# Two layer joints laid out anew: which tiles of the attention layer lie under which tiles of the recurrent layer, and in which order SyncE issues the last weight loads and the last stores

## The chip, the cores and the metric

The kernel runs on one core of a Trainium2 chip. The metric is the time of one execution on the device in microseconds (us); the median of several executions is compared.

## The reference

The program is a stack of four layers on 2048 tokens of width 640, each added to its input: A, B, A, B. Both A layers use the same weights, and so do both B layers.

```python
x = x + A(layernorm(x)); x = x + B(layernorm(x))
x = x + A(layernorm(x)); x = x + B(layernorm(x))
# A: 4 segments of 512 tokens, 32 heads of 20: causal softmax attention in the segment,
#    mixed by a gate with a linear-attention memory M, z carried over the segments; then o @ wo
# B: 64 segments of 32 tokens, 32 heads of 128
for s in range(64):
    h = concat([mem, x[32*s:32*s+32]])           # 8 memory tokens and 32 tokens
    q, k, v = h @ Wq, h @ Wk, h @ Wv
    o = softmax(mask(q @ k.T * scale)) @ v
    o = o @ Wo
    mem, out[s] = o[:8], o[8:]
```

## The kernel before, in words

**Layer A** (`layer_A`) works through 32 groups (4 segments of 8 groups of 4 heads). At its end the last segment's 512 tokens are finished as four row blocks of 128 tokens, numbered 0 to 3: `out_stage_b` multiplies each by the output weights `a_wo` (tile `a_YP`), adds the residual `a_xr` on VectorE into a 32-bit row block, stores that to the DRAM tile `xres` (line 408), makes a 16-bit copy in a slice of the tile `a_Onat` on ScalarE (line 414), and stores that to `xres_bf` (line 417). The text calls the eight stores x0, b0, x1, b1, x2, b2, x3, b3, in this order. In the first A layer the 32-bit blocks stand in `a_xnew` (block 0), `a_late` (1 and 2) and `a_xnew3` (3, in pool `a_am`); in the second in the two buffers of `a_xr` (0 and 1) and in `a_late` (2 and 3). `C.rows` holds the last eight stores.

**Layer B** (`layer_B`) is a chain of 64 steps. In a step TensorE projects K and Q (`b_Ka`, `b_Qa`, `b_Kb`, `b_Qb`, `b_Qc`), computes scores (`b_SP`) and V (`b_Va`, `b_Vb`); VectorE and ScalarE make the softmax, in which ScalarE writes `b_E` (`soft_exp`), VectorE sums it, GpSimd scales it into `b_Pn`, VectorE transposes that to `b_PTa`, `b_PTb`; TensorE then forms `b_OTP`, which goes through `b_OTsb` into 64 matmuls with the output weights (`b_OPS`). The result's first rows are the memory of the next step, so no step starts its projections before the one ahead has its `b_OPS`. In B all engines but SyncE keep the order in which the program is written (`_OrdNC`).

**Output weights of B** are eight tiles `b_wo0` to `b_wo7` of 640 KB. `WO_FIRST` = 0, 4, 1, 5, 3 is loaded first, `WO_LAST` = 7, 2, 6 last (line 889), which is the order in which `b_OPS` reads them. All loads and stores around the joints are issued by SyncE, one after the other; an issue that has to wait holds up all behind it. At a joint, order-only dependencies put the five loads of `WO_FIRST` ahead of all eight stores.

**SBUF.** Each layer opens its pools in a fixed order, and they lie one behind the other. A layer's pools begin where the pools of the layer ahead began, so each tile lies on tiles of that layer, and its first write waits until their last reader is done; the last reader can be a DMA that stores them.

Of the kernel before, what the change touches and what calls it, by code (L numbers as in the profile page):

```python
# [19 lines left out]
BF16 = mybir.dt.bfloat16  # L20
# [62 lines left out]
def layernorm_begin(nc, pool, C, xt, name):  # L83
    stats = pool.tile([128, 2, nc.vector.BN_STATS_DIM], F32, name=f"{name}_st", tag="ln_st")
    first = nc.vector.bn_stats(out=stats[:, 0, :], in_=xt[:, 0:320])
    nc.vector.bn_stats(out=stats[:, 1, :], in_=xt[:, 320:640])
    mv = pool.tile([128, nc.vector.BN_AGGR_DIM], F32, name=f"{name}_mv", tag="ln_mv")
    nc.vector.bn_aggr(out=mv[:], in_=stats[:])
    rstd = pool.tile([128, 1], F32, name=f"{name}_rstd", tag="ln_rstd")
    nc.vector.tensor_scalar(out=rstd[:], in0=mv[:, 1:2], scalar1=LN_EPS, scalar2=None, op0=ALU.add)  # L90
    nc.gpsimd.tensor_tensor(out=rstd[:], in0=rstd[:], in1=C.mhalf[:, 0:1], op=ALU.pow)
    return first, mv, rstd
# [175 lines left out]
def layer_A(nc, tc, C, W, x_src, x_dst, src_is_bf16, nseg=4, out_bf16=False, xb_dst=None, load_w=None, side_loads=None):  # L268
# [7 lines left out]
    with ExitStack() as ctx:  # L276
        def pool(name, bufs):
            return ctx.enter_context(tc.tile_pool(name=name, bufs=bufs, reuse_waits="tile"))
# [13 lines left out]
        wk = pool("a_wk", 2)  # L292
        w1 = pool("a_wk1", 1)
        stm = pool("a_stm", 1)
        pam = pool("a_am", 3)
        pon = pool("a_on", 2)
        wkl = pool("a_wkl", 2)
        w1l = pool("a_wk1l", 1)
        st = pool("a_state", 1)
        sm = pool("a_sm", 4)  # L300
        W.wo = st.tile([128, NCH, D], BF16, name="a_wo")

        def psum(name, bufs):
# [11 lines left out]
        vaug = [stm.tile([128, 4, 4, 32], BF16, name=f"a_vaug{i}") for i in range(4)]  # L315
        Kn = [stm.tile([128, 4, 4, 32], BF16, name=f"a_Kn{i}") for i in range(2)]
        phik = [ste.tile([128, 4, 4, 32], BF16, name=f"a_phik{i}") for i in range(2)]
        NM = [stm.tile([128, 4, 4, 32], BF16, name=f"a_NM{i}") for i in range(2)]

        def pads(i, eng):  # L320
            for on, dst, k in ((i < 2, Kn, 0), (True, vaug, 1)):
# [264 lines left out]
        def negmax_rows(g):  # L586
            nm, N_ = GS[g]["nm"], NM[g % 2]
            K("NM1").gpsimd.tensor_copy(N_[:, :, :, 20], nm[:])
            K("NM2").gpsimd.tensor_tensor(out=N_[:, :, :, 21], in0=nm[:], in1=N_[:, :, :, 20], op=ALU.subtract)

        def q_with_max(g):
            s_ = GS[g]
            N_ = NM[g % 2]
            Q2 = pg.tile([128, 512], F32, name="a_Q2", tag="pg")
# [111 lines left out]
        for i in range(2):  # L706
            P.memset(NM[i][:], 0.0)
            if i == 0:
# [99 lines left out]
        for g in range(NGR + 2):  # L808
            n, G = divmod(g, 8)
            for half in range(2):  # L810
                p, tp = 2 * g + half, 2 * g + half - 3
                for ph in range(2):
                    K.base = 4 * g + 2 * half + ph
                    todo = []
                    for what in VISITS[ph]:
                        kind, r = what[0], int(what[1])
# [10 lines left out]
                    for step in range(2):  # L827
                        for kind, p_, r, X, o0 in todo:
                            if step == 0 and g >= NGR and (kind, p_) != ("T", 2 * NGR - 3):
                                tail_unit(*next(PARTS))  # L830
                            f = (s_mm, s_max)[step] if kind == "S" else (t_round, t_exp)[step]
# [27 lines left out]
WO_FIRST, WO_LAST = (0, 4, 1, 5, 3), (7, 2, 6)  # L859
# [28 lines left out]
def load_B_wo(nc, W, B_Wo, k):  # L888
    return nc.sync.dma_start(W.wo[k][:], B_Wo[4 * k:4 * k + 4].rearrange("h e d -> e h d"))
# [8 lines left out]
def layer_B(nc, tc, C, W, x_src, xb_src, x_dst, mem0, B_Wv, B_Wo, nsteps=64, out_bf16=False, tag=""):  # L898
# [6 lines left out]
    with ExitStack() as ctx:  # L905
        def pool(name, bufs):
            return ctx.enter_context(tc.tile_pool(name=name, bufs=bufs, reuse_waits="tile"))
# [14 lines left out]
        for nm, ks in (("b_wo", WO_FIRST[0:3]), ("b_xo", ()), ("b_wom", WO_FIRST[3:]), ("b_wol", WO_LAST)):  # L922
# [4 lines left out]
            for k in ks:  # L927
                W.wo[k] = p_.tile([128, 4, D], BF16, name=f"b_wo{k}")
        wkl = pool("b_wkl", 1)
        wk = pool("b_wk", 1)  # L930
        sm = pool("b_sm", 2)

# [6 lines left out]
        def ps_tile(shape, dtype, name):  # L939
            return pp.tile(shape, dtype, name=name, tag="ps")  # L940
# [45 lines left out]
        def ln_begin(key, after=None):  # L986
            xt = ln_xt[key]
            f, mv, rstd = layernorm_begin(nc, sml, C, xt[:], "b_ln")
            if after is not None:
                info = mybir.DependencyInfo(mybir.DependencyClass.NoSync, mybir.DependencyReason.SCHED_ONLY)  # L990
                tc.add_manual_dep(f.ins, after.ins.name, info, reason="order")
            ln_open.append((key, xt, mv, rstd))

        def ln_end():
            if ln_open:
                key, xt, mv, rstd = ln_open.pop()
                if key[0] == "X":
                    ln_xt[key] = bx.tile([128, D], BF16, name="b_xn", tag="xt")
                layernorm_end(nc, xt[:], mv, rstd, ln_xt[key][:])
                ln_ready.append(key)  # L1000
# [16 lines left out]
        def cols_of(u):  # L1017
            return HX[u // 4][:, :, u % 4, :]
# [91 lines left out]
        for k in WO_FIRST + WO_LAST:  # L1110
            f = load_B_wo(nc, W, B_Wo, k)
            if k == WO_FIRST[-1]:
                for r in C.rows:
                    tc.add_manual_dep(r.ins, f.ins.name, mybir.DependencyInfo(mybir.DependencyClass.NoSync, mybir.DependencyReason.SCHED_ONLY), reason="order")
        ln_begin(("H", 0), C.after)
        ln_end()
        nc.vector.memset(Pn[:], 0.0)
# [74 lines left out]
        for s in range(nsteps):  # L1192
# [38 lines left out]
            negmax = sm.tile([128, 2, 5], F32, name="b_negmax", tag="negmax")  # L1231
            ssum = sm.tile([128, 2, 5], F32, name="b_ssum", tag="ssum")
            rs = sm.tile([128, 2, 5], F32, name="b_rs", tag="rs")
            E_ = wk.tile([128, 2, 5, 40], BF16, name="b_E", tag="E0")

            def soft_max(b, SP):
                nc.vector.tensor_reduce(out=negmax[:, b, :], in_=SP[:], axis=AX.X, op=ALU.max, negate=True)
# [4 lines left out]
            def soft_exp(b, SP):  # L1242
                nc.scalar.activation(out=E_[:, b], in_=SP[:], func=ACT.Exp)

            def soft_sum(b):
                nc.vector.tensor_reduce(out=ssum[:, b, :], in_=E_[:, b], axis=AX.X, op=ALU.add)

# [3 lines left out]
            def soft_p(eng, b):  # L1251
                eng.tensor_tensor(out=Pn[:, b, :, 0:40], in0=E_[:, b], in1=rs[:, b, :].unsqueeze(2).to_broadcast([128, 5, 40]), op=ALU.mult)

# [16 lines left out]
            def vtail_some(n_):  # L1270
                nonlocal vps, vc
                if work and vc < NCH:
                    vps = vtail_unit(work[0], work[1], vc, min(NCH, vc + n_), vps)
                    vc = min(NCH, vc + n_)
# [85 lines left out]
            order = [(0, 0), (0, 1), (1, 0), (1, 1), (3, 0), (3, 1), (2, 0), (2, 1)]  # L1360
# [8 lines left out]
            vtail_some(1)  # L1369
            if not last:  # L1370
                dst = cols_of(s + 1)
                msb = wk.tile([128, 320], BF16, name="b_msb", tag="msb")
                parts = ((0, 1), (1, 3), (3, NCH))
                for ca, cb in parts:
                    nc.scalar.copy(msb[:, 64 * ca:64 * cb], ops[:, 64 * ca:64 * cb])
                for pi, (ca, cb) in enumerate(parts):
                    mt = ps_tile([128, cb - ca, 8], F32, f"b_MT{pi}")
                    for c in range(ca, cb):
                        for q in range(4):
                            o = 64 * c + 32 * (q % 2)  # L1380
                            nc.tensor.matmul(mt[32 * q:32 * q + 32, c - ca, :], lhsT=msb[:, o:o + 32], rhs=selm[:, q // 2, :],
                                             start=True, stop=True, tile_position=(0, 32 * q), skip_group_check=True)
                    nc.vector.tensor_copy(dst[:, ca:cb, 24:32], mt[:])
                    vtail_some((1, 1, NCH)[pi])
# [24 lines left out]
def full_kernel(tc, A_x, A_wq, A_wk, A_wv, A_wo, A_beta, B_x, B_mem0, B_Wq, B_Wk, B_Wv, B_Wo, B_seg_len, out, layers="ABAB"):  # L1409
    nc = tc.nc  # L1410
    with ExitStack() as ctx:
        C, WA = alloc_consts(tc, ctx)
        xin = A_x.rearrange("b s d -> (b s) d")
        xout = out.rearrange("b s d -> (b s) d")
        mem0 = B_mem0.rearrange("b t d -> (b t) d")
        X = tc.dram_tile([S_TOK, D], F32, name="xres")
        Xb = tc.dram_tile([S_TOK, D], BF16, name="xres_bf")
        WB = C.WB = alloc_B_resident(tc, ctx)
        padded = {}
        stage = {nm: t_[:, k, 0:NCH * D].rearrange("p (c n) -> p c n", c=NCH)  # L1420
                 for nm, t_, k in (("wq", WB.wq, NCH - 1), ("wk", WB.wk, NCH - 1), ("wv", WB.wq, NCH - 2))}
        build_consts(nc, tc, C)
        nl = len(layers)
        assert layers[0] == "A" and layers[-1] == "B"
        for li, L in enumerate(layers):
            lastl = (li == nl - 1)
            if L == "A":
                first = li == 0

                def side(slot, after):  # L1430
                    if slot % 3 == 1 and slot // 3 < 8 * NCH:
                        load_B_resident(nc, WB, B_Wq, B_Wk, slot // 3, after)
                    if slot == 24:
                        keep_padded(nc, tc, WA, padded)

                layer_A(nc, tc, C, WA, xin if first else X, X, first, xb_dst=Xb,
                        load_w=lambda: load_A_weights(nc, tc, C, WA, A_wq, A_wk, A_wv, A_wo, padded, stage),
                        side_loads=(side, A_beta) if first else None)
            else:
                layer_B(nc, tc, C, WB, X, Xb, xout if lastl else X, mem0, B_Wv, B_Wo, out_bf16=lastl, tag=str(li))  # L1440
# [58 lines left out]
```

## Time and profile before

| | us |
|---|---|
| median of 3 runs (lowest, highest) | 2403.32 (2401.88, 2407.49) |
| profiled execution: device time | 2403.94 |
| profiled execution: span of the instructions | 2401.9 |
| first joint, A to B | about 330 to 365 in the span |
| second joint, A to B | about 1527 to 1558 in the span |

Times in the profile are microseconds from the start of the span. A row of the timeline reads: start, length, engine, line, operation, output<-inputs, shapes, count, and in brackets the idle time of the engine before it and what ended it. "SPq" rows are issues of DMAs by SyncE; their length is the time of issuing, not of the transfer. Line 114 is a helper through which most instructions are recorded, so tiles' names tell more than lines.

### The profile page before, as it was taken

What the parts mean: (1) busy time and instruction counts of PE and PEld (TensorE: products, weight loads), DVE (VectorE), ACT (ScalarE), POOL (GpSimd) and SP (SyncE); (2) the same over time, 40 slices, a digit from 0 to 9 for tenths busy, and PEclk for the clock granted to TensorE, in tenths of its full rate; (3) what the DMA queues carried; (4) which work ended last, traced back from release to release, by engine and by line L of the source; (5) the groups of instructions that cost most, each with busy time, mean ns of one, the idle gap of its engine ahead of it and who ended that gap; (6) DMA issues with size and microseconds to landing.
All of it is one profiled execution on the core that took longest, in us unless ns stands there. A gap on an engine that the chain in (4) does not pass through costs nothing.

```text
span 2401.9 us, 139146 instructions
## 1 busy us (share of the span) xinstructions
PE 2274.9 (95%) x62200; PEld 1491.3 (62%) x62264; DVE 1882.6 (78%) x4701; ACT 1414.2 (59%) x3194; POOL 749.2 (31%) x1590
## 2 busy tenths in 40 slices
PE   8999989999999999999989999899999999999998
PEld 5566655666666666666656665566666666666665
DVE  9999876777777777777789998777777777777776
ACT  6999964445444445444479999644544444444443
POOL 6677741111111111111146776311111111111111
PEclk9999999999999999999999999999999999999999
DMA  5122271111111111111130211711111111111110
GB/s 169 50 86 67 72 255 25 29 33 29 32 29 30 31 31 32 29 29 29 45 113 19 68 51 34 270 25 26 28 29 26 28 27 27 27 29 28 27 23 21
DMA packets 173186, 123.37 MB, mean 51 GB/s; under 512 B 106652, under 2 KB 157740, under 8 KB 171052
## 3 DMA queue, kind: packets, MB, share of 16 engines
q1 hardware_dynamic: 172162, 114.44, 16.6%
q8 instruction: 486, 7.96, 1.4%
q14 instruction: 112, 0.92, 0.1%
q10 hardware_dynamic: 426, 0.05, 0.0%
HBM read 79.60 MB, written 34.80 MB: 48 GB/s over the span
## 4 chain that ended last, share of the span: by engine, by line
PE 70%; DVE 14%; ACT 9%; DMA 3%; issue 3%; POOL 1%; SPq 0%; ACTq 0%; POOLq 0%; DVEq 0%
PE b_OPS L114 11%; PE b_Ka L114 6%; PE b_Qa L114 6%; PE b_Kb L114 6%; DVE a_nm L143 5%; PE b_tail L114 5%; PE b_Vb L114 5%; PE b_Va L114 5%; ACT a_PT L143 4%; PE b_vtail L114 3%; PE b_OPSd L114 3%; PE b_SP L114 3%; PE a_S L114 3%; PE b_OTP L114 2%; PE b_Qb L114 2%
## 5 line engine op out<-in xcount | busy, mean ns | idle before, releaser
L114 POOL TENSOR_TENSOR b_Pn<-b_E,b_rs 128x200 bf16<-128x200 bf16 x256 | 133.5, 522 | 1084.7 <-DVE b_rs L114 1067.0
L143 DVE TENSOR_REDUCE a_nm<-a_S 128x2 f32<-128x512 f32 (+3 forms) x512 | 395.0, 815 | 44.4 <-PE a_S L114 29.3
L143 ACT ACTIVATE a_PT<-a_T 128x1024 bf16<-128x1024 f32 (+1 forms) x384 | 345.7, 905 | 23.4 <-PE a_T L114 16.5
L114 PEld LDWEIGHTS <-b_HX 128*32 128x32 bf16 x9200 | 239.1, 96 | 140.0 <-DVE b_HX L114 3.0
L114 PEld LDWEIGHTS <-b_R 128*32 128x32 bf16 x8960 | 231.9, 96 | 138.9 <-DVE b_R L114 3.1
L114 PE MATMUL b_OPS<-b_wo,b_OTsb 128*32 128x320 bf16 x8192 | 306.6, 300 | 5.9 <-issue 4.8
L114 PEld LDWEIGHTS <-b_OTsb 128*32 128x32 bf16 x8192 | 207.8, 97 | 75.4 <-DVE b_OTsb L114 20.7
L114 DVE STREAM_TRANSPOSE b_KT<-b_kq 128x512 bf16<-128x512 bf16 x256 | 181.4, 708 | 84.8 <-ACT b_kq L114 80.7
L143 POOL TENSOR_SCALAR_AFFINE_SELECT a_PT<-a_PT 128x256 bf16<-128x256 bf16 x380 | 188.9, 502 | 149.5 <-ACT a_PT L143 143.4
L114 ACT ACTIVATE b_E<-b_SP 128x200 bf16<-128x200 f32 x256 | 86.3, 337 | 235.1 <-DVE b_SP L114 224.1
L114 PEld LDWEIGHTS <-c_J 128*32 128x32 bf16 (+1 forms) x5760 | 180.2, 96 | 63.8 <-issue 10.8
L114 DVE STREAM_TRANSPOSE b_QT<-b_kq 128x256 bf16<-128x256 bf16 (+1 forms) x384 | 184.0, 504 | 39.0 <-ACT b_kq L114 35.8
L114 ACT CAST b_msb<-b_OPS 128x64 bf16<-128x64 f32 x378 | 69.3, 256 | 217.4 <-PE b_OPS L114 217.4
L114 DVE CAST b_OTsb<-b_OTP 128x160 bf16<-128x160 f32 (+1 forms) x384 | 133.8, 376 | 43.0 <-PE b_OTP L114 38.4
L114 ACT CAST b_kq<-b_Ka 128x512 bf16<-128x512 f32 x128 | 74.9, 585 | 125.1 <-PE b_Ka L114 125.1
L114 PE MATMUL b_vtail<-b_wv,c_J 128*32 128x256 bf16 x2560 | 141.9, 273 | 0.3
L114 ACT CAST b_OTsb<-b_OTP 128x320 bf16<-128x320 f32 x256 | 96.5, 429 | 76.8 <-PE b_OTP L114 76.5
L114 PEld LDWEIGHTS <-b_Vth 32*128 32x128 bf16 x4096 | 74.9, 91 | 94.1 <-ACT b_tu L114 37.2
L114 PE MATMUL a_T<-a_q,a_kT 32*128 32x512 bf16 (+3 forms) x1024 | 120.2, 299 | 11.1 <-DVE a_nm L143 5.8
L114 PEld LDWEIGHTS <-c_identb 128*32 128x32 bf16 (+1 forms) x1886 | 94.9, 97 | 44.3 <-issue 14.2
L114 PE MATMUL b_OPSd<-b_wo,b_OTdef 128*32 128x320 bf16 x2048 | 114.1, 299 | 2.8 <-issue 2.7
L114 PE MATMUL a_S<-a_kT,a_qT 32*128 32x256 bf16 (+3 forms) x1024 | 113.6, 299 | 1.9 <-ACT a_kT L143 1.6
(214 smaller groups left out, 5393.3 us busy)
## 6 DMA issues: line engine op xcount, KB each, us to landing
b_wv<-in_B_Wv_dram SPq DMA_DIRECT2D x10, 1024.0 KB
b_wo<-in_B_Wo_dram SPq DMA_DIRECT2D x16, 640.0 KB
b_VT<-b_VTd SPq DMA_DIRECT2D x504, 16.0 KB
b_XO<-xres SPq DMA_DIRECT2D x256, 30.0 KB
b_VTd<-c_J SPq DMA_DIRECT2D x480, 16.0 KB
b_xt<-xres_bf SPq DMA_DIRECT2D x38, 160.0 KB
b_wk<-in_B_Wk_dram SPq DMA_DIRECT2D x20, 256.0 KB
b_wq<-in_B_Wq_dram SPq DMA_DIRECT2D x20, 256.0 KB
```

The costliest lines, as they stand in the source:

```text
L114: r = f(*a, **k)
L143: r = f(*a, **k)
```

## The change

Three things are moved, no instruction is added or taken out.

1. The pools of A get another order: `a_sm` (small statistics) moves up, the pool `a_on` (`a_Onat`, `a_late`) moves down behind `a_wo`, the two `a_NM` tiles get a pool behind that, and `a_am` comes last.
2. In B the tiles `b_E` and `b_msb` move from pool `b_wk` to a new pool `b_wke` just ahead of it.
3. The loads of `WO_LAST` get order-only dependencies that put them ahead of the last four stores (x2, b2, x3, b3) on SyncE.

```diff
         stm = pool("a_stm", 1)
-        pam = pool("a_am", 3)
-        pon = pool("a_on", 2)
+        sm = pool("a_sm", 4)
         wkl = pool("a_wkl", 2)
         w1l = pool("a_wk1l", 1)
         st = pool("a_state", 1)
-        sm = pool("a_sm", 4)
+        pon = pool("a_on", 2)
+        pnm = pool("a_nmp", 1)
+        pam = pool("a_am", 3)
...
-        NM = [stm.tile([128, 4, 4, 32], BF16, name=f"a_NM{i}") for i in range(2)]
+        NM = [pnm.tile([128, 4, 4, 32], BF16, name=f"a_NM{i}") for i in range(2)]
...
         wkl = pool("b_wkl", 1)
+        wke = pool("b_wke", 1)
         wk = pool("b_wk", 1)
...
             if k == WO_FIRST[-1]:
                 for r in C.rows:
                     tc.add_manual_dep(r.ins, f.ins.name, ...)
+            if k in WO_LAST:
+                for r in C.rows[4:]:
                     tc.add_manual_dep(r.ins, f.ins.name, ...)
...
-            E_ = wk.tile([128, 2, 5, 40], BF16, name="b_E", tag="E0")
+            E_ = wke.tile([128, 2, 5, 40], BF16, name="b_E", tag="E0")
...
-                msb = wk.tile([128, 320], BF16, name="b_msb", tag="msb")
+                msb = wke.tile([128, 320], BF16, name="b_msb", tag="msb")
```

Summing the tiles' sizes in the pools' order gives where they lie, in bytes of a partition from the start of the layers' pools. At the first joint (the second differs by the sizes of a few tiles, and the tiles of B lie 640 bytes higher):

| tile of A, last segment | before | after |
|---|---|---|
| `a_NM` | 86528 to 88576 | 113344 to 115392 |
| `a_am` (`a_oTx`, `a_oTx`, `a_xnew3`) | 88576 to 96256 | 115392 to 123072 |
| `a_late` | 96256 to 101376 | 103104 to 108224 |
| `a_Onat` (four blocks of 1280 bytes) | 101376 to 106496 | 108224 to 113344 |
| `a_xr`, `a_oT` | 106496 to 111616 | 87552 to 92672 |
| `a_xnew` | 111616 to 114176 | 92672 to 95232 |
| `a_wo` | 115456 to 121856 | 96512 to 102912 |

| tile of B | before | after |
|---|---|---|
| `b_wo7`, `b_wo2`, `b_wo6` | 86784, 91904, 97024 to 102144 | the same |
| `b_OTdef`, `b_Vth`, `b_PTa`, `b_PTb`, `b_OTsb` | 102144 to 112128 | the same |
| `b_E`, `b_msb` | 118784 to 120224 | 112128 to 113568 |
| `b_KT`, `b_VT`, `b_QT` | 112128 to 118784 | 113568 to 120224 |

At the second joint `a_Onat` lies at 108032 to 113152 after the change, `b_E` at 112768 to 113568, the two `a_xr` buffers at 87552 to 92672, and `b_wo7` at 87424 to 92544.

More of the change, by code (lines that the diff above doesn't have):

```diff
@@ L1114, in layer_B @@
                     tc.add_manual_dep(r.ins, f.ins.name, mybir.DependencyInfo(mybir.DependencyClass.NoSync, mybir.DependencyReason.SCHED_ONLY), reason="order")
+            if k in WO_LAST:
+                for r in C.rows[4:]:
+                    tc.add_manual_dep(r.ins, f.ins.name, mybir.DependencyInfo(mybir.DependencyClass.NoSync, mybir.DependencyReason.SCHED_ONLY), reason="order")
         ln_begin(("H", 0), C.after)
```

## The prediction

> **What bounds the kernel now.** I read the page first, then the timeline at the two joints, the chain of waits at the second joint, the list of DMAs and windows of granted clock.
>
> ```profile
> span 2401.9 us, 139146 instructions
> PE 2274.9 (95%) x62200; PEld 1491.3 (62%) x62264; DVE 1882.6 (78%) x4701; ACT 1414.2 (59%) x3194; POOL 749.2 (31%) x1590
> PE 70%; DVE 14%; ACT 9%; DMA 3%; issue 3%; POOL 1%; SPq 0%; ACTq 0%; POOLq 0%; DVEq 0%
> ```
>
> TensorE (PE) is busy 95% of the span, and the chain that ended last lies on it for 70%. B is a chain of steps, so a microsecond that a joint loses or wins moves everything behind it. DMA has 3% of the chain, and the joints are where it can enter. The first joint:
>
> ```profile
> 340.08 1.31 SPq L408 DMA_DIRECT2D xres<-a_xnew  x1
> 341.30 1.53 PE L114 MATMUL a_YP<-a_wo,a_oTx 128*128 128x320 bf16 x10
> 349.35 0.71 DVE L114 STREAM_TRANSPOSE b_KT<-b_kq 128x512 bf16<-128x512 bf16 x1 [3.66 <-DMA xres<-a_xnew]
> 350.06 3.66 SPq L889 DMA_DIRECT2D b_wo<-in_B_Wo_dram  x3
> 352.78 0.34 ACT L114 ACTIVATE b_E<-b_SP 128x200 bf16<-128x200 f32 x1 [1.23 <-DVE b_SP L114]
> 356.96 1.25 PE L114 MATMUL b_OPS<-b_wo,b_OTsb 128*32 128x320 bf16 x29
> 362.23 2.59 PE L114 MATMUL b_OPS<-b_wo,b_OTsb 128*32 128x320 bf16 x35 [4.01 <-issue]
> 365.59 1.26 PE L114 MATMUL b_Ka<-b_wk,b_R 128*32 128x512 bf16 x20
> ```
>
> The reader sees three things. b_KT lies on a_xnew, whose store x0 was issued at 340.08, and VectorE waits for it until 349.35. The last three weight loads go out only from 350.06 to 353.72. And PE stands still for 4.01 in the middle of the first b_OPS, with no releaser named ("issue"); b_OPS ends at 362.23 + 2.59 = 364.82. The second joint, its timeline and then its chain:
>
> ```profile
> 1546.31 0.32 SPq L417 DMA_DIRECT2D xres_bf<-a_Onat  x1
> 1547.55 4.03 SPq L889 DMA_DIRECT2D b_wo<-in_B_Wo_dram  x3
> 1549.38 0.34 ACT L114 ACTIVATE b_E<-b_SP 128x200 bf16<-128x200 f32 x1 [1.26 <-DVE b_SP L114]
> 1554.61 2.08 PE L114 MATMUL b_OPS<-b_wo,b_OTsb 128*32 128x320 bf16 x56
> 1557.45 0.46 PE L114 MATMUL b_OPS<-b_wo,b_OTsb 128*32 128x320 bf16 x8 [0.77 <-DMA b_wo<-in_B_Wo_dram]
> ...
> 1534.26 10.25 DMA b_wo<-in_B_Wo_dram
> 1544.57 6.02 DMA xres<-a_late
> 1550.64 0.38 SPq L889
> 1551.13 6.28 DMA b_wo<-in_B_Wo_dram
> ```
>
> Here the chain runs over transfers: store x3 takes 6.02 from issue to landing, the last load can be issued only behind it and behind b3 (at 1551.13), lands at 1557.41, and PE waits 0.77 for it. b_OPS ends at 1557.45 + 0.46 = 1557.91. These are queues of bytes:
>
> ```profile
> 333.00:343.00 10.00, 8.62 (x84) 4.55 (x76) 7.89 (x21) 3.56 (x9) 0.55 (x1) 1.00 1.03 382
> 343.00:349.00 6.00, 6.00 (x153) 4.12 (x150) 2.04 (x5) 4.07 (x9) 0.40 (x1) 1.00 1.06 378
> 1540.00:1548.00 8.00, 8.00 (x234) 5.68 (x227) 4.29 (x9) 5.34 (x12) 0.74 (x2) 1.00 1.06 379
> ...
> b_wo<-in_B_Wo_dram SPq DMA_DIRECT2D x16, 640.0 KB
> xres<-a_late SPq DMA_DIRECT2D x4, 320.0 KB
> xres_bf<-a_Onat SPq DMA_DIRECT2D x8, 160.0 KB
> ```
>
> The last two numbers of a window are the busy share of the 16 DMA engines and GB/s: full, at about 380. So at both joints transfers queue, and what is put ahead of a store delays its landing by its bytes.
>
> **The change part by part.** *What goes.* b_KT no longer lies on rows that are being stored (it lies on a_NM and an a_oTx, read by engines only), so VectorE's 3.66 goes. b_wo6 lies on a_wo, which is dead when the last a_YP ends (341.30 + 1.53 = 342.83), instead of on a_Onat and a_late. So the weights come sooner, and the 0.77 at the second joint goes.
>
> *What is late next.* The table of bytes says that b_E now lies on the last block of a_Onat: at the first joint b_E's 112128 to 112928 fall into block 3 (112064 to 113344), at the second its 112768 to 113568 begin inside block 3 (111872 to 113152). That block is being stored by b3, the last store of all. Before, b_E lay on a_wo. So ScalarE's first b_E of each layer B gets a wait for b3, and b3 has just been put behind three loads of 640 KB. Behind b_E in ScalarE's order stand the second b_E and the copies of V; VectorE's sums, GpSimd's b_Pn, the transposes and PE's b_OTP and b_OPS wait for its result. PE has only b_Va, b_Vb and one b_tail left to do meanwhile, then idles.
>
> *When b3 lands, first joint.* Before, the third load's issue ended at 353.72; it takes about 0.4 (the 0.38 row), and it waited for b3, so b3 landed by 353.3. The loads are 3 x 655,360 bytes at 380 bytes/ns = 5.2. SyncE can issue b_wo2, which lies partly on a_xnew, only when x0 has landed (349.3, as before, since nothing ahead of x0 moves), but b0, x1, b1 and b_wo7 keep the engines busy in the meantime. So b3 lands at 353.3 + 5.2 = 358.5, 5.7 after b_E's 352.78.
>
> *Second joint.* b3 landed before by 1551.1. x2, b2, x3, b3 are 983,040 bytes, 2.6 at 380, so b1 had landed at 1548.5 and x1 (b1's 160 KB less) at 1548.1. In this layer b_wo7 lies on both a_xr buffers, which hold x0 and x1 until these are stored, so SyncE holds b_wo7, and all behind it, until 1548.1, and the queue runs dry. How long a transfer takes in a quiet queue:
>
> ```profile
> 1168.84 1.64 SPq L1152 DMA_DIRECT2D xres<-b_XO  x2
> 1171.01 1.67 SPq L1202 DMA_DIRECT2D b_XO<-xres  x2
> ```
>
> The load at 1171.01 had to wait for the first store, issued at 1168.84: 2.2 for 30 KB, nearly all fixed. So b3 lands at about 1548.1 + 2.2 + 5.2 + 2.6 = 1558.1; bounds 1556.3 (1551.1 + 5.2, no dry stretch) and 1559.5 (x1 later and a slower engine).
>
> *From b_E to the end of b_OPS.* The second step, where all is there in time, and the clock after PE's 4.01 of idling:
>
> ```profile
> 372.02 0.34 ACT L114 ACTIVATE b_E<-b_SP 128x200 bf16<-128x200 f32 x1 [1.49 <-DVE b_SP L114]
> 374.39 0.20 PE L114 MATMUL b_OTP<-b_PTa,b_Vth 32*128 32x40 bf16 x4 [0.40 <-DVE b_PTa L114]
> 375.60 2.38 PE L114 MATMUL b_OPS<-b_wo,b_OTsb 128*32 128x320 bf16 x64
> ...
> 362.20:364.80 2.60, 2.58 (x39) 1.44 (x39) 0.00 (x0) 0.00 (x0) 0.00 (x0) 0.50 0.08 19
> 365.60:368.80 3.20, 3.20 (x72) 1.60 (x64) 2.07 (x6) 1.55 (x3) 0.00 (x0) 1.00 0.11 25
> ```
>
> Warm, b_OPS ends 375.60 + 2.38 - 372.02 = 6.0 after b_E starts; in the first joint b_E to b_OPS took 4.18 instead of 3.58, so 6.6 is possible. But after 4.01 of idling the granted clock was 0.50 for at least 2.6 and 1.00 again 3.4 later, and 35 matmuls took 2.59 (74 ns each against 37 in the row of 64). PE will idle about 5 at either joint, so I take 3.0 of half clock from the first b_OTP (2.4 after b_E): until 5.4, with b_OPS starting at 4.0; 1.4 / 0.074 = 19 matmuls slow, 45 x 0.037 = 1.7 fast, end at 7.1. Upper bound, all slow: 4.2 + 64 x 0.074 = 8.9.
>
> The Trainium skill, "TensorE: Matmul & The Clock Gate", section "What's actually happening", says that the clock halves after an idle window of about 3.4 us and comes back after about 3.4 of sustained work. The trace agrees on the halving; by the page's 3.4 instead of my 3.0 the end is 0.2 later at each joint.
>
> *The sum.* First joint: 358.5 + 7.1 = 365.6 against 364.82, +0.8; the 4.01 of PE is gone or swallowed by the new wait, which is longer. Second: 1558.1 + 7.1 = 1565.2 against 1557.91, +7.3. Together +8.1. The profiled execution took 2403.94, so 2412.0; the median lies 0.62 lower, so 2411.4. Bounds: 357.5 + 6.0 and 1556.3 + 6.0 give -1.3 + 4.4 = +3.1; 360 + 8.9 and 1559.5 + 8.9 give +4.1 + 10.5 = +14.6.
>
> *At nothing.* The other new overlays are read by engines that are done before the writer comes: b_wo3 on a_sm, b_KT and b_VT on a_oTx. At the first joint b_rs touches a_xnew3, but x3 lands ahead of b3 and b_rs is written after b_E. b_VTd, b_XO and b_xt come later on SyncE, by at most the 5 us of b3, and are first needed a step later. At the joint from B to A, a_NM now lies on tiles of B that die before the last b_OPS:
>
> ```profile
> 1207.98 0.52 POOL L143 MEMSET a_NM<- 128x512 bf16 x1 [4.41 <-PE b_OPS L114]
> ```
>
> GpSimd may start this sooner, but nothing waits for it there; a_wo, now on b_wo2 and b_wo6, must wait for B's last b_OPS, and it is needed a whole segment later.
>
> **The rivals.** *A, faster: the stores are down when b_E comes.* If b3's landing is not held up by the loads, or b_E's address is not where I put it, the joints only win: 4.01 and the slow clock behind it (2.59 - 35 x 0.037 = 1.3) at the first, 0.8 at the second, together 6.1: 2397.2 in the median. For it: the 4.01 stands among full DMA queues, and before the change b3 came at 353.3, close to b_E. Against: full queues at 380 GB/s. It decides where the two landings of b3 together are 8.1 earlier than I say; below that the change wins.
>
> *B, no difference: stores overtake loads.* The Trainium skill, "DMA: Bandwidth & Descriptors", section "Queues, rings and completion order", says that completion is not in order of issue over an issuing engine, though each DMA engine takes its ring in order. As a mechanism here: part of the stores' packets slip past the loads, b3 lands some 4 before my times, both joints win and lose alike: b_OPS ends at 361.6 and 1561.2, -3.2 + 3.3 = 0, 2403.4. Against: x3 took 6.02 from issue, which is the bytes ahead of it.
>
> *C, slower still:* PE's 4.01 has no named cause; if it comes again behind the new wait, with the half clock prolonged, add 4 to 5: 2416.
>
> **How the numbers follow.** Forecast 0.70, A 0.13, B 0.11, C 0.06. A measurement of this kernel can tell about 0.2% (4.8 us) from no change. The forecast's own range is 2406.4 to 2416; a tenth of it falls inside 4.8. So slower 0.70, same 0.17, faster 0.13. The range that leaves out A and the ends: 2402.5 to 2416.
>
> **What would show it.** Right: b_E of the first step idles for `DMA xres_bf<-a_Onat` at 358 and 1558; PE has a gap of 4 to 7 ahead of b_OTP with clock 0.50 after it; b_KT no longer waits for a store; x2 to b3 are issued behind three b_wo; b_OPS waits for no b_wo. Wrong: b_E starts at 352 and 1549 as before, or b_OPS ends before 364 and 1560.

## The result, and the profile after

| | before | after |
|---|---|---|
| median (lowest, highest) of 6 and 6 runs, us | 2405.22 (2401.88, 2407.65) | 2417.26 (2414.32, 2420.14) |
| ratio after to before, 95% interval | | 1.0054 (1.0043 to 1.0065) |
| profiled execution: device time, span, us | 2403.94, 2401.9 | 2420.14, 2418.1 |

The change made the kernel 12.0 us slower. The forecast was slower by 8.1, 2411.4 in the median, with a range up to 2416.0: the sign and the mechanism hold, the size is a third short. The page after, the lines that answer to those of before:

```profile
span 2418.1 us, 139132 instructions
...
PE 2281.3 (94%) x62200; PEld 1493.5 (62%) x62264; DVE 1882.6 (78%) x4701; ACT 1413.9 (58%) x3194; POOL 749.2 (31%) x1590
...
PE 70%; DVE 13%; ACT 10%; DMA 2%; issue 2%; POOL 1%; SPq 1%; ACTq 0%; POOLq 0%; DVEq 0%
```

The shares hardly move, because 12 us are 0.5% of the span; the joints have to be read by themselves. The first joint, its timeline:

```profile
343.63 1.53 PE L114 MATMUL a_YP<-a_wo,a_oTx 128*128 128x320 bf16 x10
...
345.89 6.86 SPq L890 DMA_DIRECT2D b_wo<-in_B_Wo_dram  x3
...
350.35 0.71 DVE L114 STREAM_TRANSPOSE b_KT<-b_kq 128x512 bf16<-128x512 bf16 x1 [2.32 <-ACT b_kq L114]
...
354.87 0.85 SPq L418 DMA_DIRECT2D xres_bf<-a_Onat  x1
...
360.31 0.61 PE L114 MATMUL b_Vb<-b_wv,b_R 128*32 128x512 bf16 x7 [4.17 <-issue]
...
362.46 0.56 ACT L114 ACTIVATE b_E<-b_SP 128x200 bf16<-128x200 f32 x2 [8.46 <-DMA b_XO<-xres]
...
364.74 0.22 PE L114 MATMUL b_OTP<-b_PTa,b_Vth 32*128 32x40 bf16 x4 [1.87 <-DVE b_PTa L114]
...
366.10 4.49 PE L114 MATMUL b_OPS<-b_wo,b_OTsb 128*32 128x320 bf16 x64
```

b_KT waits for no store any more. The three b_wo go out ahead of b3 (issued at 354.87), ScalarE idles 8.46 ahead of b_E until 362.46, and b_OPS ends at 366.10 + 4.49 = 370.59. The releaser named there, a load of b_XO, is not the one: b_E waits for the semaphores on which all four stores of a_Onat run, b0 to b3, and this load was issued later on the semaphore of b1. The last of the four to land was b3, whose last part came at 362.28. The profile as a whole lies later than before's, so positions are told from the end of the last a_YP from here on: 342.83 before, 345.17 after at this joint (a hundredth is lost in the rows' rounding). b_OPS ended 21.98 after it, and now 25.42. The second joint:

```profile
1544.99 1.53 PE L114 MATMUL a_YP<-a_wo,a_oTx 128*128 128x320 bf16 x10
...
1554.71 1.48 SPq L890 DMA_DIRECT2D b_wo<-in_B_Wo_dram  x3
...
1558.23 0.38 SPq L418 DMA_DIRECT2D xres_bf<-a_Onat  x1
...
1566.22 0.57 ACT L114 ACTIVATE b_E<-b_SP 128x200 bf16<-128x200 f32 x2 [11.50 <-DMA xres_bf<-a_Onat]
...
1568.51 0.22 PE L114 MATMUL b_OTP<-b_PTa,b_Vth 32*128 32x40 bf16 x4 [10.18 <-DVE b_PTa L114]
...
1569.86 3.74 PE L114 MATMUL b_OPS<-b_wo,b_OTsb 128*32 128x320 bf16 x64
```

Here the chain is as forecast, store by store: SyncE stands until x1 has landed, b3 lands at 1566.12, b_E follows, TensorE (PE) has waited 10.18, b_OPS ends at 1573.60. That is 27.08 after the last a_YP instead of 17.99. The joints lose 3.44 and 9.09, together 12.5, about the difference of the medians (12.0). The two profiled executions are 16.2 apart, but 2.3 of that lies ahead of the first joint, where the changed kernel's second profile (e5, below) shows none of it (342.97). Windows of the same trace: PE, PEld, DVE, ACT, POOL busy, then the granted clock, the busy share of the DMA engines, and GB/s:

```profile
349.00:352.00 3.00, 3.00 (x71) 1.61 (x62) 1.27 (x2) 1.32 (x4) 0.00 (x0) 1.00 1.04 390
352.00:355.00 3.00, 2.62 (x128) 2.12 (x120) 2.23 (x6) 1.24 (x3) 0.00 (x0) 1.00 0.96 303
...
1553.00:1557.00 4.00, 4.00 (x156) 3.03 (x152) 3.24 (x8) 1.31 (x3) 0.00 (x0) 1.00 0.34 93
...
1560.00:1562.00 2.00, 0.00 (x0) 0.00 (x0) 0.00 (x0) 0.00 (x0) 0.00 (x0) 1.00 0.95 219
...
361.00:364.70 3.70, 1.87 (x19) 0.60 (x12) 1.56 (x7) 2.02 (x5) 1.14 (x3) 0.50 0.31 84
...
370.00:371.00 1.00, 0.90 (x24) 0.26 (x12) 0.00 (x0) 0.36 (x3) 0.00 (x0) 0.50 0.00 0
...
1571.00:1572.00 1.00, 1.00 (x22) 0.56 (x18) 0.00 (x0) 0.00 (x0) 0.00 (x0) 0.50 0.12 33
1572.00:1573.00 1.00, 1.00 (x24) 0.67 (x20) 0.00 (x0) 0.00 (x0) 0.00 (x0) 0.64 0.05 16
```

The queues are not full throughout: 303 GB/s at 352 to 355, 93 at 1553 to 1557, and 219 at 1560 to 1562, in the middle of the loads, although the engines count as busy. And the clock is still 0.50 at the end of b_OPS at 370 to 371.

### The profile page after: what moved, and what is told of

It is laid out like the page before. It is cut to its first block, busy times and chain, and to the rows that moved or that the text cites. A ratio compares the mean times of both kernels' runs of the same rounds, so it can differ in the third digit from the quotient of the medians.

```text
span 2418.1 us, 139132 instructions
## 1 busy us (share of the span) xinstructions
PE 2281.3 (94%) x62200; PEld 1493.5 (62%) x62264; DVE 1882.6 (78%) x4701; ACT 1413.9 (58%) x3194; POOL 749.2 (31%) x1590
## 4 chain that ended last, share of the span: by engine, by line
PE 70%; DVE 13%; ACT 10%; DMA 2%; issue 2%; POOL 1%; SPq 1%; ACTq 0%; POOLq 0%; DVEq 0%
PE b_OPS L114 11%; PE b_Ka L114 6%; PE b_Qa L114 6%; PE b_Kb L114 6%; DVE a_nm L143 5%; PE b_Va L114 4%; PE b_tail L114 4%; PE b_Vb L114 4%; ACT a_PT L143 4%; PE b_vtail L114 4%; PE b_OPSd L114 3%; PE b_SP L114 3%; PE a_S L114 3%; PE b_OTP L114 2%; PE b_Qc L114 2%; PE b_Qb L114 2%
## 5 line engine op out<-in xcount | busy, mean ns | idle before, releaser
L114 DVE TENSOR_TENSOR b_XO<-b_OPS,b_XO 64x320 f32<-64x320 f32 x192 | 92.9, 484 | 33.1 <-DMA b_XO<-xres 28.1
```

Source lines behind the costliest of these rows:

```text
L114: r = f(*a, **k)
```

## The experiments

The kernels were timed in several groups; the kernel before had medians of 2402 to 2412 in them, so each ratio is to the kernel before timed beside it. Positions are microseconds after the end of the last a_YP of the joint, in one profile of each kernel.

| kernel | b_E starts, joints 1, 2 | b_OPS ends, joints 1, 2 | sum of ends | ratio (95%) |
|---|---|---|---|---|
| before, first profile | 9.95, 9.46 | 21.98, 17.99 | 39.97 | |
| before again (e10) | 10.07, 9.46 | 20.31, 17.34 | 37.65 | 1.0004 (0.9994 to 1.0015) |
| after, first profile | 17.30, 19.70 | 25.42, 27.08 | 52.50 | 1.0054 (1.0043 to 1.0065) |
| after again (e5) | 17.11, 19.26 | 24.31, 26.97 | 51.28 | 1.0059 (1.0047 to 1.0071) |
| e1 stores first | 10.67, 10.50 | 17.91, 20.44 | 38.35 | 1.0004 (0.9995 to 1.0013) |
| e2 b_E elsewhere | 10.08, 9.46 | 23.13, 25.14 | 48.27 | 1.0031 (1.0019 to 1.0044) |
| e3 order at joint 1 only | 16.82, 10.92 | 24.23, 20.46 | 44.69 | 1.0021 (1.0010 to 1.0031) |
| e4 b_OTdef last | 10.94, 10.97 | 18.98, 20.32 | 39.30 | 1.0005 (0.9996 to 1.0013) |
| e6 one load ahead | 12.23, 15.70 | 20.20, 23.60 | 43.80 | 1.0036 (1.0024 to 1.0048) |
| e7 TensorE kept busy | 16.80, 19.62 | 23.71, 25.39 | 49.10 | 1.0062 (1.0047 to 1.0077) |
| e8 pages moved | 11.01, 12.12 | 21.95, 19.49 | 41.44 | 1.0035 (1.0021 to 1.0049) |
| e9 fewer bytes | 10.50, 11.26 | 16.72, 17.03 | 33.75 | 0.9983 (0.9975 to 0.9991) |
| e11 pages moved otherwise | 10.67, 11.42 | 22.45, 20.47 | 42.92 | 1.0012 (1.0002 to 1.0021) |
| e12 mixed, exchanged | 10.08, 14.05 | 19.30, 21.29 | 40.59 | 1.0001 (0.9989 to 1.0013) |
| e13 mixed | 10.62, 9.46 | 19.99, 18.13 | 38.12 | 1.0001 (0.9988 to 1.0014) |
| e14 other order of loads | 15.97, 19.04 | 23.78, 26.92 | 50.70 | 1.0047 (1.0035 to 1.0059) |
| e15 b_wo6 first | 16.12, 19.64 | 23.13, 27.28 | 50.41 | 1.0048 (1.0034 to 1.0062) |

Counted from the mean of the two profiles of before (38.8), the sums agree with the ratios to about 2 us, except in e6, e7 and e8, whose ratios are 3.7, 4.6 and 5.8 us above their sums. These three were timed beside the same executions of the kernel before, as was e5 (1.7 above); the cause is not known.

**Is it the order?** e5 is the changed kernel again. e1 takes the order out and leaves the layout:

```diff
-            if k in WO_LAST:
-                for r in C.rows[4:]:
-                    tc.add_manual_dep(r.ins, f.ins.name, ...)
```

> The changed kernel itself, unaltered, on the same chip as the runs beside it. In its first profile b_OPS of step 0 ends 25.4 and 27.1 after the last a_YP at the two joints, against 22.0 and 18.0 in the kernel before, 12.5 in all; every theory expects a ratio near 1.0052, and the same two joints.

> The changed kernel's layout, but the order-only dependency that puts the last weight loads ahead of x2 to b3 is taken out, so the stores go first as before the change. Theory (b_E lies on the block that b3 stores, and the loads delay b3): b3 lands by 353 and 1551 again, the first b_E starts within 2 us of that, b_OPS ends near 360 at the first joint and near 1557.6 at the second, counted as in the kernel before; the median is about 2400, some 17 below the changed kernel. Rival 1 (the layout itself costs, by slower stretches in layer A or by TensorE's unnamed stalls): it stays at 2412 to 2417. Rival 2 (without the new order the weights are what is late): b_OPS waits for b_wo and the median is 2405 or more.

e1 is level with the kernel before: without the order nothing is left of the 12 us, so neither the layout's effect on layer A nor late weights make the loss (both rivals fall). But e1 is not 5 us faster than before, as I expected. (The order was not run on the old layout: by the table of bytes b_wo6 lies there on a_late and a_Onat, so that its load has to come behind their stores.) b_OPS there:

```profile
355.51 0.61 PE L114 MATMUL b_Vb<-b_wv,b_R 128*32 128x512 bf16 x7 [1.70 <-issue]
...
358.19 2.55 PE L114 MATMUL b_OPS<-b_wo,b_OTsb 128*32 128x320 bf16 x64
...
1561.16 0.21 PE L114 MATMUL b_OTP<-b_PTb,b_Vth 32*128 32x40 bf16 x1 [2.41 <-issue]
...
1561.80 3.44 PE L114 MATMUL b_OPS<-b_wo,b_OTsb 128*32 128x320 bf16 x64
```

The first joint ends 4.1 earlier than in the first profile of before (and 2.4 earlier than in the second), the second 2.5 later: PE stands 2.41 there with no releaser named, and b_OPS takes 3.44 instead of 2.55. What is won at one joint is lost at the other.

e3 keeps the order at the first joint only (`if k in WO_LAST and tag == "1"`):

> The changed kernel with the new order kept at the first joint only; at the second the stores go ahead of the last loads again. Theory (+3.4 at the first joint and +9.1 at the second in the traces): the second joint loses its cost, and the median is about 2408, some 9 below the changed kernel. Rival (the joints cost alike, or the rest lies in the layers): 2411 to 2413.

As expected: 1.0021, and the second joint alone drops from about 27 to 20.46.

**Is it b_E, and the bytes ahead of b3?** e2 moves b_E of step 0 alone; e6 puts one load ahead instead of three (`if k == WO_LAST[0]`).

```diff
-            E_ = wke.tile([128, 2, 5, 40], BF16, name="b_E", tag="E0")
+            E_ = wke.tile(...) if s else C.J[:, 640:1040].rearrange("p (b g k) -> p b g k", b=2, g=5)
```

> The changed kernel, with b_E of step 0 alone put into a scratch tile that nothing stores (later steps as in the change). Theory: the wait at b_E goes, b_E starts near 352 and 1550, but b_OTsb still touches the first 64 bytes of the block that b3 stores, so the copies into b_OTsb wait for the same store, some 2.7 us further down the step; saved are at most 2.7 at each joint: about 2412. Rival 1 (b_E's overlay is the whole cost): 2406 or less. Rival 2 (the cost is TensorE's own stall, or late weights): no change, 2417.

> The changed kernel with one of the three last loads (b_wo7) ahead of x2 to b3 instead of three. Theory (each 640 KB put ahead of the stores delays b3 by 1.72 at 380 GB/s, and b_E with it; the halt that wo7 makes at the second joint stays): b_E starts about 3.5 earlier than in the changed kernel at both joints, near 13.6 and 16.2 after the last a_YP; b_OPS ends near 20.6 and 23.6, 8.3 less than the changed kernel; about 0.0018 above the kernel before. Rival 1 (the delay is the dry queue at the halt and not the bytes): b_OPS ends within 2 of the changed kernel at each joint. Rival 2 (the order costs only by TensorE's stalls): b_E moves but b_OPS stays.

In e2 b_E runs on time and little is won, 1.2 and 1.8: the next overlays wait for the same store. They are not b_OTsb, as I had it, but ScalarE's b_Vth and VectorE's b_PTa already, at the second joint of e2 (and, at the first, b_rs for x3):

```profile
360.43 0.19 DVE L114 RECIPROCAL b_rs<-b_ssum 128x5 f32<-128x5 f32 x1 [5.10 <-DMA xres<-a_xnew]
...
1566.84 0.58 ACT L114 CAST b_Vth<-b_Va 128x512 bf16<-128x512 f32 x1 [8.78 <-DMA xres_bf<-a_Onat]
1566.86 0.57 DVE L114 STREAM_TRANSPOSE b_PTa<-b_Pn 128x256 bf16<-128x256 bf16 x2 [8.18 <-DMA xres_bf<-a_Onat]
```

b_PTa lies on the first two blocks of a_Onat there, whose stores are done early, and yet it starts 0.1 after b3, whose last part landed at 1566.74. So a tile waits for the last reader of the whole tile beneath it, not of the block: b_E would have waited for b3 anywhere on a_Onat, and my reading of the byte ranges was finer than the wait is. b_rs on a_xnew3, which the prediction put at nothing because b_E comes first, waits as soon as b_E is out of the way.

In e6 b_E comes 4.9 and 3.6 earlier than in e5, b_OPS 4.1 and 3.4: 1.7 to 2.4 for each load of 640 KB. The dose decides for the stores behind the loads, and the rival that only the dry queue counts falls. The ratio, 1.0036, is higher than the 1.0018 I expected and than the joints account for.

**The part of the landing that was short.** e14 issues the loads as 7, 6, 2 at the first joint and 2, 6, 7 at the second, e15 as 6, 7, 2 at the second.

> The changed kernel with the last three loads issued in another order, still all ahead of x2 to b3: 7, 6, 2 at the first joint and 2, 6, 7 at the second, so that the one which has to wait for a store (b_wo2 on a_xnew, b_wo7 on a_xr) comes last and the queues hold two loads meanwhile. Theory (the halt leaves the queues dry for 2 to 3 at the second joint and about 1 at the first, over and above the bytes): b3 lands and b_E starts about 2.2 earlier at the second joint (near 17.0 after the last a_YP instead of 19.2) and 1 earlier at the first, b_OPS ends as much earlier; ratio about 1.0046. Rival (only the bytes count, or the halt lets the stores already issued land sooner, so that nothing is lost): b_E where it was, 17.1 and 19.3, ratio 1.0059.

> As the run with the last loads in another order (7, 6, 2 at the first joint), but with 6, 7, 2 at the second: b_wo2 reaches 128 bytes into the second a_xr buffer there, so with 2 first the halt stayed where it was (b_E at 19.0); b_wo6 lies on no store. Theory (the dry queue behind the halt costs over and above the bytes): one load of 640 KB, 1.7 at 380 GB/s, fills part of the 3 dry, so b3 and b_E come 1.7 earlier at the second joint, near 17.4 after the last a_YP; the first joint as there (b_E near 16); b_OPS ends near 23.8 and 25.2, ratio about 1.004. Rival (only the bytes ahead of b3 count at the second joint): b_E stays near 19.2.

At the first joint this settles it. With b_wo2 last the queue stays full (387 and 376 GB/s in the two windows that had 390 and 303), and b_E starts at 15.97, 1.1 earlier than in e5. At the second e14 changed nothing, because b_wo2 reaches 128 bytes into a_xr and SyncE halts all the same. In e15 b_E still comes only at 19.64, but for another reason. Windows of e15:

```profile
1552.00:1558.00 6.00, 1.62 (x32) 0.65 (x24) 0.10 (x1) 0.00 (x0) 0.00 (x0) 0.96 1.02 342
1558.40:1559.70 1.30, 0.00 (x0) 0.00 (x0) 0.00 (x0) 0.00 (x0) 0.00 (x0) 0.50 0.07 26
```

15 of the 16 parts of b3 had landed at 1558.73, 17.57 after the last a_YP, where the theory had it (17.4). From 1558.4 on the share is 0.07, which is one engine of 16, working off packets alone; the sixteenth part landed at 1560.70. So in this one profile the load ahead of the halt brought 15 parts of b3 forward by 1.3 (in e5 they had landed at 18.91), and one late engine gave it back. b_E itself stayed where the rival has it, so the theory is borne out here by the 15 parts alone. Why that engine was late was not tried.

**The clock.** e7 adds matmuls that nobody reads ahead of the first b_OTP:

```diff
+            if s == 0:
+                W_ = po.tile([128, 512], F32, name="b_W", tag="opsd")
+                for _ in range(6 if tag == "1" else 42):
+                    nc.tensor.matmul(W_[:], lhsT=C.identb[:], rhs=W.wk[:, 0, 0:512], ...)
             otf = [ps_tile(...
```

> The changed kernel with matmuls added whose result nobody reads, ahead of the first b_OTP of step 0: 6 of 512 columns at the first joint, 42 at the second, about the length of TensorE's wait there. Theory (b_OPS at half clock after the wait is part of the cost): at the second joint b_OPS takes 2.4 instead of 3.7 and ends 1.3 to 2 earlier; at the first joint, where TensorE has stood still in b_Vb before, at most 1 earlier; 2 to 3 in all, ratio 1.0042. Rival (the clock plays no part, the matmuls are slow for want of weights or of the queue): b_OPS takes 3.7 as before, no difference or slower.

```profile
1562.88 0.20 PE L114 MATMUL b_OTP<-b_PTa,b_Vth 32*128 32x40 bf16 x4 [0.70 <-DVE b_PTa L114]
...
1563.98 2.39 PE L114 MATMUL b_OPS<-b_wo,b_OTsb 128*32 128x320 bf16 x64
```

b_OPS takes 2.39 instead of 3.7 to 4.1, and the second joint ends 1.6 earlier, the first 0.6. So the half clock is part of the cost, as forecast. 2.2 of 2415 is too little for the ratio to show; it came out at 1.0062, and the 1.0042 that I expected lies below its interval.

**PE's stalls with no releaser.** In all kernels but e8 and e11 the stalls of this kind begin at fixed places of PE's own program, counted in matmuls and weight loads from the last a_YP: at the 351st, 607th and 864th at the first joint, at the 507th and 765th at the second, 256 to 258 apart, whatever waits there. A row of the profile after the change (queue, kind, packets, MB) goes with it:

```profile
q8 instruction: 486, 7.96, 1.4%
```

62,200 matmuls and 62,264 weight loads in 486 packets are 256 for each packet of 16 KB. The Trainium skill, "Runtime: NRT & Kernel Launch", section "Instruction fetch mechanics", says that an engine's program comes in blocks of 16 KiB, 256 instructions, over a DMA queue of its own while the block ahead runs, and that this is mostly hidden. The row agrees with the block; at these joints it is not hidden. e9 loads a quarter of the last three weights and leaves out the rest, so that its result is another; e10 is the kernel before again, e8 and e11 shift the blocks.

```diff
-    return nc.sync.dma_start(W.wo[k][:], B_Wo[4 * k:4 * k + 4]...)
+    n_ = 1 if k in WO_LAST else 4
+    return nc.sync.dma_start(W.wo[k][:, 0:n_], B_Wo[4 * k:4 * k + n_]...)
```

> Stores first, as in the run without the new order, and of each of the last three weight loads only the first head's quarter (160 instead of 640 KB); the products of the other three heads read that quarter too, so 1.4 MB less is moved at each joint and the output is another. Theory (TensorE stands still at a page of 256 instructions because its fetch waits among full DMA queues): in the run without the new order a page came 5 to 7 after the one ahead was entered; with the queues empty from about 12 on it comes in 3 or less, the stalls of 1.7 at the 607th instruction of the first joint and of 2.4 at the 765th of the second shrink below 0.6, b_OPS ends near 16.3 and 16.8 after the last a_YP instead of 17.9 and 20.4, ratio about 0.998. Rival (the fetch has a fixed time, whatever the queues hold): the stalls stay at 1.5 to 2.5 and nothing is gained.

> The kernel before itself, for a second profile of it. In its first one TensorE stood still for 4.01 in the first joint's b_OPS, where the page at the 864th instruction begins. Theory (fetch among full queues): a stall at the same instructions again, 607th and 864th and, at the second joint, 507th and 765th, of a size that varies from run to run; b_OPS ends between 18 and 22 at the first joint, near 18 at the second. Rival (the 4.01 was an accident of one run): no stall over 1 at the first joint, b_OPS ends near 17.5. Ratio 1.000.

e9, the first joint's stall and both b_OPS:

```profile
354.95 0.61 PE L114 MATMUL b_Vb<-b_wv,b_R 128*32 128x512 bf16 x7 [0.61 <-issue]
...
357.62 2.56 PE L114 MATMUL b_OPS<-b_wo,b_OTsb 128*32 128x320 bf16 x64
...
1554.24 2.38 PE L114 MATMUL b_OPS<-b_wo,b_OTsb 128*32 128x320 bf16 x64
```

The stalls of 1.70 and 2.41 shrink to 0.61 and nothing. In the trace of DMA packets, the packet of a block starts 1.0 to 1.6 after PE has entered the block ahead, from the 351st and the 507th instruction of e9 on; with fuller queues it took up to 4.1 in e1, 4.7 after the change and 5.7 before it. In all profiles a stall of this kind ends 1.1 to 1.6 after its packet is through. e10 has the stall of the first profile at the same instruction, of another size:

```profile
361.55 1.64 PE L114 MATMUL b_OPS<-b_wo,b_OTsb 128*32 128x320 bf16 x35 [2.37 <-issue]
```

So the 4.01 before the change was a late fetch, on the high side: 1.7 of the first joint's 21.98 did not come again and was luck of that execution.

> Stores first, as in the run without the new order, and TensorE's instruction stream made longer ahead of the joints by small matmuls whose result nobody reads: 92 of 8 columns before the first projection of the first A, and in the second A the 30 matmuls that are there for the clock cut into 106 narrower ones. Theory of the unnamed stalls (in the runs so far they begin at the 351st, 607th and 864th TensorE instruction after the last a_YP at the first joint and at the 507th and 765th at the second, 256 to 258 apart whatever the kernel's order: each page of 256 instructions is fetched through the DMA engines, which are full): the stalls move by the added instructions, to about the 423rd and 680th at both joints; the one at the 765th (2.4) and the half clock behind it go, and the second joint ends 2 to 3 earlier, the first up to 1; a ratio of about 0.9985. Rival (a stall belongs to what is read there, the operands or a semaphore): it stays in b_Vb and in the second b_OTP, with no gain.

> As the run with longer instruction streams, but without the 92 small matmuls in the first A: only the second joint's pages move, by 152 instructions, to where the first joint has them (355th, 612th, 869th). Theory: the first joint ends near 17.9 as in the run without the new order, the second near 18 instead of 20.4, because it gets the first joint's stall in b_Vb (1.7) in place of the one in b_OTP (2.4) and no half clock in b_OPS; ratio about 0.999. Rival (the place of the page is of no account, the total wait for pages is the same): 20 or more at the second joint, ratio 1.0005 or more.

The expectations have the two A layers exchanged: the clock's matmuls stand in the first A, the 92 were added in the second. By that the first joint's blocks moved by 152 instructions in both kernels, the second's by 336 in e8 and 152 in e11. The stalls went where this puts them (e8, then e11):

```profile
359.29 0.22 PE L114 MATMUL b_OTP<-b_PTa,b_Vth 32*128 32x40 bf16 x3 [2.79 <-issue]
```

```profile
1562.57 1.86 PE L114 MATMUL b_OPS<-b_wo,b_OTsb 128*32 128x320 bf16 x33 [2.50 <-issue]
```

At the first joint from b_Vb into b_OTP (711th), at the second into b_OPS (868th in e11) or just behind PE's wait for b_PTa, by whose end the packet was there, and none is seen (e8). The mechanism is shown, but moving the blocks won nothing: the stall at the first joint grew (2.79 and 3.63) and brought the half clock into b_OPS.

**Is there a kernel better than both?** e4 takes the order out and moves b_OTdef behind b_E, so that b_E lies on blocks stored early; e12 and e13 have the new layout at one joint and the old at the other.

> Stores first, as in the run without the new order, and the b_OTdef tiles moved from ahead of b_Vth to behind b_E and b_msb: they are written at the end of step 0 only, so they take the place on a_Onat's later blocks, and b_E moves up onto a_Onat's first block, which is stored early. Theory: b_E needs to wait neither at 349 nor at 1549.4; what comes last is b_wo6 (about 358 and 1556.5), b_OPS ends near 358.5 and 1557: about 2398, which would beat both kernels. Rival (the wait goes over to the next overlays, b_PTb and b_OTsb on a_late, or TensorE's stall comes again): 2401 to 2404.

> The new layout at the first joint, the old one at the second, stores first at both: for each joint what ended earlier so far. Theory: b_OPS ends near 17.9 at the first joint (no store waits ahead of b_KT, 22.0 in the kernel before) and near 18.0 at the second, as in the kernel before; 1.5 to 4 less than that: ratio 0.9985 to 0.9993. Rival (the old first joint's 4.01 was an accident, and nothing is won without it): 1.000.

> The new layout at the first joint, the old one at the second, stores first at both; the run called e12 had the layouts of layer A the wrong way round (old ahead of the first joint, new ahead of the second, with b_E's place the other way). Theory: b_OPS ends near 17.9 to 19 after the last a_YP at the first joint (20.3 and 22.0 in the two profiles of the kernel before; no store waits ahead of b_KT) and near 17.5 to 18 at the second: 2 to 3 less than the kernel before, ratio 0.9988. Rival (what the first joint wins at b_KT is lost again to the fetch of TensorE's pages, which comes at its own pace): b_OPS ends at 20 or later at the first joint, ratio 1.000.

No: 1.0005, 1.0001 and 1.0001. In e4 b_E still waits for b3, which landed at 10.79 and 10.74 and was followed by b_E at 10.94 and 10.97: again the whole tile counts, and lying on early blocks brings nothing. e12 was built with layer A's layouts exchanged, and has a wait for b_QT of 4.04 at the second joint. e13 is the one that was meant; its first joint loses 3.08 to a block, its second 1.52 to b_wo6:

```profile
356.72 0.61 PE L114 MATMUL b_Vb<-b_wv,b_R 128*32 128x512 bf16 x7 [3.08 <-issue]
...
1557.31 0.46 PE L114 MATMUL b_OPS<-b_wo,b_OTsb 128*32 128x320 bf16 x8 [1.52 <-DMA b_wo<-in_B_Wo_dram]
```

Its rival holds: what the first joint wins at b_KT goes to the fetch. Only e9, which leaves out 1.4 MB of weights at each joint and is no replacement, is faster.

## Why the prediction was right in kind and short in size

*Right.* b_E of the first step waits for b3 at both joints (by the tile, where I argued by the block); b_KT's wait is gone; the three loads stand ahead of x2 to b3; SyncE takes up b_wo7 at the second joint 8.2 after the last a_YP, as forecast (1548.1 less 1539.91); b_OPS waits for no weights; the second joint carries most of the loss (9.1, forecast 7.3). e1, e3 and e6 show that the order makes it on this layout. One sign was off: PE's gap ahead of b_OTP was 10.18 at the second joint, where I had said 4 to 7, because b_E came 10.2 later there than before (19.70 against 9.46) and PE had little else to do.

*Wrong: two terms of the sum.* In positions after the last a_YP the forecast had b_OPS's ends at 22.77 and 25.29; they came at 25.42 and 27.08, 2.65 and 1.79 later. That is the 4.4 by which +8.1 falls short of 12.5.

1. b3's landing, "353.3 + 5.2" and "1548.1 + 2.2 + 5.2 + 2.6": 15.67 and 18.19 forecast, 17.11 and 19.59 measured, 1.4 short at each joint. Counted in before's times b3 landed at 359.9 and 1559.5, just at the prediction's upper bounds, of which it gives no reason for the 360. At the first I wrote that b0, x1, b1 and b_wo7 keep the engines busy until b_wo2 goes out. They did not (303 GB/s from 352 to 355), and e14, which has the bytes without the halt, has b_E at 15.97, close to my 15.67. At the second joint the dry queue is not what was short: SyncE took up b_wo7 when I had said, and about 2.3 later the queue was full again. Two later stretches ran slower than the full rate that the sum has for them:

```profile
1554.65:1557.00 2.35, 2.35 (x95) 1.53 (x80) 1.95 (x6) 0.07 (x1) 0.00 (x0) 1.00 0.35 78
1557.00:1560.00 3.00, 1.32 (x28) 0.48 (x16) 0.00 (x0) 0.00 (x0) 0.00 (x0) 1.00 1.08 379
1560.00:1562.00 2.00, 0.00 (x0) 0.00 (x0) 0.00 (x0) 0.00 (x0) 0.00 (x0) 1.00 0.95 219
1562.00:1565.00 3.00, 0.00 (x0) 0.00 (x0) 0.00 (x0) 0.00 (x0) 0.00 (x0) 0.58 1.04 396
1565.00:1566.10 1.10, 0.00 (x0) 0.00 (x0) 0.00 (x0) 0.00 (x0) 0.00 (x0) 0.50 0.57 195
```

For two microseconds in the middle of the loads the engines were as busy but moved little more than half as much, and in the last 1.1 the rate fell off. Against 380 that costs 0.85 and 0.5, about the 1.4. Why the loads' packets took longer from 1560 to 1562 is open.
2. From b_E to the end of b_OPS, 7.1 forecast: 8.13 and 7.38 measured. I let the half clock last 3.0 from the first b_OTP. At the second joint it lasted about 4; at the first until 371, more than 6 after the first b_OTP, and all 64 matmuls of b_OPS ran slow (4.49). The first joint's size is partly this execution's own: in e5 the half clock ended 3.8 and 4.9 after the first b_OTP and the term was 7.19 and 7.72. The clock moves in steps: in all 17 profiles each stretch at 0.50 between the ends of the program lasted 3.4, 6.8 or 10.2. Three such steps of the first profile's first joint, then the single one of e5:

```profile
361.00:364.40 3.40, 1.87 (x19) 0.60 (x12) 1.26 (x5) 1.94 (x5) 0.84 (x2) 0.50 0.32 87
364.40:367.80 3.40, 2.94 (x100) 2.08 (x103) 2.43 (x8) 0.84 (x3) 1.25 (x4) 0.50 0.07 14
367.80:371.20 3.40, 3.30 (x64) 1.80 (x59) 0.05 (x1) 0.55 (x3) 0.00 (x0) 0.50 0.07 14
```

```profile
362.77:366.18 3.41, 3.24 (x80) 2.13 (x84) 1.69 (x5) 0.75 (x2) 0.50 (x2) 0.50 0.07 14
```

In all 17 profiles the clock came back behind a step in which PE was busy for 2.8 or more of the 3.4; it stayed low behind steps with up to 2.5, and once behind more, the 2.94 here. The "TensorE: Matmul & The Clock Gate" page of the Trainium skill, section "What's actually happening", has 3.4 of sustained work for the way back. The rows agree with 3.4 as the step; where a step was broken by long waits, another had to follow.

*The range and the base.* The sum's own upper ends, +14.6, held the result; the range stops at 2416, where rival C lay, and the prediction gives no other reason for it. Of the 5.9 between 2411.4 and 2417.26, 3.9 is the size; 1.9 is the kernel before, whose median rose from 2403.32 to 2405.22 with three more executions. The first joint of before also ended late by luck in the profile that I counted from: against e10 the same forecast ends would give +10.4, and e5 less e10 is 13.6. C's condition came true in part: the stall came again (4.17), but ahead of b_E's wait, so that only its clock cost anything. Rivals A and B fall: b3 landed late, and behind the loads. A's price was wrong too: with the stores in time (e1), 6.1 should have been won and none was, because the stall is no property of the old layout but a fetch among full queues, and because b_E waits for b3 in e1 too, if only until 10.67 and 10.50.

## What to carry to other kernels

Before a tile is laid over another, ask who reads any part of the old one last: a store that an engine's first write must wait for landed here only behind all the bytes queued ahead of it, so loads should not be put ahead of stores on whose tiles the next step's engines write. When the bytes ahead are counted, count also the time in which the issuing engine stands and the queue runs dry, and do not take the full rate up to the last byte. A stall with no releaser that sits at the same count of instructions in every variant, 256 apart, was here the program being fetched. It was longer the fuller the DMA queues were, and taking bytes out of such a stretch (e9) brought more than moving the instructions (e8, e11).

## What the runs showed that I had not expected

- TensorE's program comes through the same full DMA engines: up to 5.7 us from the entry of one block of 256 instructions to the packet of the next, against 1.0 to 1.6 in e9, and stalls of up to 4.7 us (e7, first joint).
- One DMA engine of 16 can end a store behind the other 15, 2.0 us in e15 and 0.9 in e2 (second joint), and the waiting engine sees only the last.
- The granted clock stayed at 0.50 for 10.2 us at the first joint, from 361 to 371, though PE was busy for 7.9 of the 10 between; in the second profile of the same kernel it was 3.4.
- The rate of full DMA queues fell to 219 GB/s for 2 us in the middle of the loads, with the engines counted as busy (1560 to 1562).
